# Where three normalizes stand in VectorE's queue: operand differences and an add moved ahead of them in the second chunks

## The chip, the cores and the metric

The kernel runs on one core of one Trainium2 chip. The metric is the device time of one execution in microseconds (us), as a median over several runs. TensorE does the matrix products, VectorE and ScalarE empty the accumulation banks (PSUM) and do the elementwise work, GpSimd and SyncE issue the transfers. Each engine works through its own queue in the order in which the program gives it its instructions. An instruction that waits holds up all that stands behind it on the same engine.

## The reference

Attention with projected keys and values, followed by a feed-forward layer with a squared ReLU:

```python
def _attn_ref(q, k, v, E, F):                 # q, k, v: 8 x 8 x 1024 x 64; E, F: 64 x 1024
    k_proj = np.einsum('ks,bhsd->bhkd', E, k)
    v_proj = np.einsum('ks,bhsd->bhkd', F, v)
    scores = np.matmul(q, k_proj.transpose(0, 1, 3, 2)) / np.sqrt(64)
    attn = softmax(scores)                    # over the 64 projected keys
    return np.matmul(attn, v_proj)

def _moe_ref(x, w_in, w_out):                 # x: 8192 x 512, w_in: 512 x 2048, w_out: 2048 x 512
    h = np.maximum(x @ w_in, 0.0)
    return h * h @ w_out
```

The heads of the attention's output are laid side by side as the 512 columns of `x`. Inputs and output are float32.

## The kernel before, in words

**Batches and chunks.** The outer loop runs over the eight batches b = 0 to 7. While TensorE does the feed-forward layer of batch b, pieces of the attention of batch b+1 (and a few of b+2) are put between its steps. A batch of 1024 tokens is two chunks of 512. The feed-forward work of a batch is a list of 62 steps, numbered from 0: for b of 1 and more these are 16 first-layer steps of chunk 0 (0 to 15), 15 second-layer steps of chunk 0 (16 to 30), then the same for chunk 1: first layer 31 to 46, second layer 47 to 61. The "second chunks" of this case are the steps 47 to 61.

**Order.** The order on every engine is written out by hand: instructions stand in each engine's queue in the order in which the program issues them. The dictionaries `PIECES` (batches 2 to 5), `BATCH_2` (used in batch 1's list), `LAST_PIECES` (batch 6) say ahead of which step each attention piece is issued. A piece at key n is issued just before step n.

**First layer.** A step is four matmuls of 128x512 into a bank. ScalarE takes the ReLU (lines 561 and 563), VectorE squares the result into `hsq` (line 571).

**Second layer.** The product of the 512 squared tokens with `w_out` is done with Strassen's scheme in Winograd's form: seven half-size products instead of eight. It needs four sums of blocks of `hsq`, called `s[0]` to `s[3]`, which VectorE makes in `sums` (line 521), each in two halves of four of the eight blocks: the low half (`q4` = 0) during the first layer, the high half (`q4` = 1) at its end or in the second layer. In this kernel they depend on one another: `s[1]` reads `s[0]`, `s[3]` reads `s[1]`, `s[2]` reads only `hsq`. Three are differences; `s[0]` is a sum. The products are the steps `p1` to `p7`, most of them split into a low and a high half (`lo`, `hi`), each half 8 matmuls of 128x256 (line 527). `p6` reads `s[1]`, `p5` reads `s[0]`, `p7` reads `s[2]`, `p3` reads `s[3]`. The orders of the second chunk are:

```python
# b = 1: steps 47 to 61
[p1a, p2a, p1b, p1c] + lohi(p5) + lohi(p6) + lohi(p3) + lohi(p7) + [p2b]  + lohi(p4)
# b = 2 to 6
[p1a, p2a, p1b, p1c, p2b] + lohi(p6) + lohi(p5) + lohi(p7) + lohi(p3)  + lohi(p4)
```

So for b = 2 to 6 step 51 is `p2b`, 52 and 53 are `p6`, 54 and 55 `p5`, 56 and 57 `p7`, 58 and 59 `p3`, 60 and 61 `p4`; for b = 1 step 48 is `p2a`, 49 `p1b`, 50 `p1c`, 51 and 52 `p5`, 53 and 54 `p6`, 55 and 56 `p3`, 57 and 58 `p7`, 59 `p2b`.

**Banks.** The products are accumulated in three banks called x, y and z. In batches 2 to 6 x and z are the same bank: `p2b` finishes x, VectorE's add (line 657, `o_sb` from `ps_z` and `p_a`) takes it into the output tile, and `p5` then starts z in that same bank. `p_a` is ScalarE's copy of y after `p1c` (line 651). y goes the same way: VectorE's add of y and `p_d` after `p7` frees y for `p4`.

**The attention pieces here.** `values g e` (line 258) multiplies the softmax's numerators with the projected values into a two-bank attention tile; `normalize g e` (line 285) multiplies that tile with the reciprocal sums `rs` on VectorE and writes a quarter of `xT`, the next batch's feed-forward input. A normalize frees its attention tile. In batch 1 there are two such tiles, so `values 1 0` and `values 1 1` (step 55) take the tiles that `normalize 0 0` and `normalize 0 1` read. From batch 2 on there are three.

Of the kernel before, what the change touches and what calls it, by code (L numbers as in the profile page):

```python
# [20 lines left out]
def kernel(  # L21
# [166 lines left out]
    class Attention:  # L188
# [262 lines left out]
            "+copy_vp, exponentials 2, +copy_kp",  # L451
        19: "exponentials 3", 20: "+copy_v_down", 21: "+transpose_q",
        27: "sums 0, sums 1, values 0 0, reciprocals 0", 28: "reciprocals 1", 29: "normalize 0 0",
        49: "values 0 1, values 1 0, values 1 1", 51: "normalize 0 1", 53: "normalize 1 0",
        55: "normalize 1 1",
    }
    LAST_PIECES = {
        18: "scores 0, scores 1, scores 2", 20: "exponentials 0, exponentials 1", 21: "exponentials 2",
        23: "scores 3, exponentials 3",
        27: "sums 0, sums 1, values 0 0, reciprocals 0", 28: "reciprocals 1", 29: "normalize 0 0",  # L460
        49: "values 0 1, values 1 0, values 1 1", 51: "normalize 0 1", 53: "normalize 1 0",
        55: "normalize 1 1",
    }
    BATCH_1 = {
# [10 lines left out]
        24: "scores 0, scores 1, exponentials 0", 25: "exponentials 1",  # L475
        27: "scores 2, scores 3, exponentials 2", 28: "exponentials 3",
        30: "sums 0, sums 1, logs 0", 31: "logs 1", 
        33: "+transpose_q, inverses 0", 36: "inverses 1", 47: "values 0 0, values 0 1", 48: "normalize 0 0, normalize 0 1",
        55: "values 1 0, values 1 1, +project 1", 56: "normalize 1 0",
        58: "+copy_kp", 59: "+copy_vp, normalize 1 1", 61: "+copy_v_down",  # L480
    }
# [22 lines left out]
    def ffn_groups(b, xT):  # L504
# [7 lines left out]
        def sums(hsq, s, q4, which):  # L512
            js = slice(4 * q4, 4 * q4 + 4)
            a11, a21 = hsq[:, 0, js, 0:TH], hsq[:, 0, js, TH:TCH]
            a12, a22 = hsq[:, 1, js, 0:TH], hsq[:, 1, js, TH:TCH]
            for o, x, y, op in (
                (0, a21, a22, ALU.add), (1, s[0][:, js], a11, ALU.subtract),
                (2, a11, a21, ALU.subtract), (3, a12, s[1][:, js], ALU.subtract),
            ):
                if o in which:  # L520
                    nc.vector.tensor_tensor(out=s[o][:, js], in0=x, in1=y, op=op)  # L521

        def product(ps, lhs, rhs, js, first=False, tbs=range(2)):

            for tb in tbs:
                for n, j in enumerate(js):
                    nc.tensor.matmul(  # L527
                        ps[tb] if len(ps) == 2 else ps[0][:, tb], lhsT=lhs[:, j, tb * P:(tb + 1) * P],
                        rhs=rhs[:, j], start=first and n == 0 and (tb == 0 or len(ps) == 2), stop=True,
                        skip_group_check=True,  # L530
                    )
# [3 lines left out]
        def chunk(ch):  # L535
# [49 lines left out]
            def operands(q4, which):  # L585
                sums(st["hsq"], st["s"], q4, which)
# [60 lines left out]
            def copy(to, name):  # L647
                if not (last and name == "y"):
                    used(f"ps_{name}")
                for ps, t in parts(st[name]):  # L650
                    nc.scalar.copy(to[:, t], ps)  # L651
# [18 lines left out]

            def p2a():
                if b:
                    operands(1, (1,) if b > 1 else (1, 3, 2))
                product(st["x"], st["A12"], W21, before, True)

            def p1b():
# [1 line left out]

            def p1c():
                product(st["y"], st["A11"], W11, range(7, 8))  # L680
                st["a"] = part_pool.tile([P, 2, MH], F32, name="p_a")
                copy(st["a"], "y")

# [51 lines left out]
            if 1 < b < B - 2 and ch == 0:  # L735
                second = [p1a, p1b, p1c, p2a, p2b] + lohi(p6) + lohi(p5) + lohi(p7) + lohi(p3)
            elif b == B - 1:
                (p5a, p5b), rest = lohi(p5), lohi(p7) + lohi(p3)
                second = [p1a, p2a, p5a, p1b, p1c, p2b] + lohi(p6) + [p5b] + rest
            elif b > 1:  # L740
                second = [p1a, p2a, p1b, p1c, p2b] + lohi(p6) + lohi(p5) + lohi(p7) + lohi(p3)
            else:
                second = [p1a, p2a, p1b, p1c] + lohi(p5) + lohi(p6) + lohi(p3) + lohi(p7) + [p2b]
# [88 lines left out]
```

## Time and profile before

| | |
|---|---|
| median of 4 runs | 482.97 us (482.19 to 484.17) |
| the profiled execution's own time | 483.14 us |
| its span | 481.4 us |
| granted TensorE clock | 0.999 |
| PE (TensorE's matmuls) busy | 468.3 us, 97% of the span |
| DVE (VectorE) busy | 314.2 us, 65% |
| ACT (ScalarE) busy | 247.8 us, 51% |
| POOL (GpSimd) busy | 34.9 us, 7% |

The profile is one execution of the program. PE is TensorE's matmul side and PEld its weight loads, DVE is VectorE, ACT is ScalarE, POOL is GpSimd, SP is SyncE. Matmuls are pipelined, and their ends in the profile are modelled: a row of 16 matmuls of 128x256 that run without a pause is listed as 1.91 us long, while the next such row starts 1.75 us after it. A pause of TensorE between two products is therefore best read from the distance of their starts, or from the chain, which lists a row from one end to the next. The chain is the path of work that ended last, followed back from the last instruction of the program; a step of it can be on any engine.

### The profile page before, as it was taken

The numbers are of one execution on the slowest core, as the hardware profiler recorded it, in microseconds if no ns is written. First come the engines' busy times: TensorE is split into PE (matmuls) and PEld (weight loads), VectorE is DVE, ScalarE is ACT, GpSimd is POOL, SyncE is SP. The second block draws the span as 40 slices with busy tenths as digits, with TensorE's granted clock in tenths as the row PEclk, the third lists the DMA queues.
The fourth block names the chain that finished last, engine by engine and source line by source line (L and its number), as shares of the span: only waits on it lengthen the run. The fifth ranks groups of instructions, "written<-read, shape, count | busy, mean of one in ns | idle before, by whom it ended". The sixth has DMA issues, their size and how long they took to land.

```text
span 481.4 us, 8400 instructions
## 1 busy us (share of the span) xinstructions
PE 468.3 (97%) x3630; PEld 293.9 (61%) x3630; DVE 314.2 (65%) x382; ACT 247.8 (51%) x365; POOL 34.9 (7%) x48
## 2 busy tenths in 40 slices
PE   3899999999999999999999999999999999999997
PEld 2544687475664756748475574846657475766656
DVE  1578955554957659584694837857485856949383
ACT  2377535758516574375633756156652666334352
POOL 6440020020020100001000100000000000000000
PEclk9999999999999999999999999999999999999999
DMA  9999989569979998209952199223401002020202
GB/s 163 203 204 207 154 187 200 139 111 221 159 125 238 141 205 149 88 1 143 229 78 89 14 182 213 43 87 58 130 1 75 13 1 88 1 89 0 89 1 87
DMA packets 72789, 55.46 MB, mean 115 GB/s; under 512 B 33968, under 2 KB 64944, under 8 KB 72752
## 3 DMA queue, kind: packets, MB, share of 16 engines
q0 software_dynamic: 30624, 29.36, 39.5%
q1 hardware_dynamic: 42128, 25.56, 21.0%
q8 instruction: 28, 0.46, 0.4%
q14 instruction: 9, 0.07, 0.0%
HBM read 59.24 MB, written 16.78 MB: 158 GB/s over the span
## 4 chain that ended last, share of the span: by engine, by line
PE 92%; DVE 4%; ACT 2%; DMA 1%; issue 0%; SPq 0%
PE ps_h L507 27%; PE ps_y L527 21%; PE ps_att L507 17%; PE ps_z L527 15%; PE ps_kv L216 2%; PE ps_att L527 2%; PE ps_att L258 2%; PE ps_att L243 2%; DVE hsq L571 1%; DMA e_f<-in_F_dram 1%; PE ps_x L527 1%; DVE s L521 1%; ACT h_relu L561 1%; PE ps_k L301 1%; DVE xT L285 0%; ACT expT L353 0%
## 5 line engine op out<-in xcount | busy, mean ns | idle before, releaser
L571 DVE TENSOR_TENSOR hsq<-h_relu 128x1024 bf16<-128x1024 f32 x123 | 149.9, 1222 | 79.1 <-ACT h_relu L563 62.5
L507 PEld LDWEIGHTS <-w_in 128*128 128x128 bf16 x1024 | 99.8, 98 | 117.6 <-issue 1.9
L507 PE MATMUL ps_h<-xT,w_in 128*128 128x512 bf16 x640 | 147.8, 379 | 0.2 <-DVE xT L390 0.2
L527 PEld LDWEIGHTS <-s 128*128 128x128 bf16 x1024 | 99.1, 98 | 17.2 <-issue 5.1
L561 ACT ACTIVATE h_relu<-ps_h 128x512 f32<-128x512 f32 x159 | 92.3, 596 | 24.0 <-PE ps_h L507 23.8
L507 PE MATMUL ps_att<-xT,w_in 128*128 128x512 bf16 x384 | 90.7, 379 | 0.0
L527 PEld LDWEIGHTS <-hsq 128*128 128x128 bf16 x768 | 73.8, 98 | 16.4 <-issue 6.0
L563 ACT ACTIVATE h_relu<-ps_att 128x1024 f32<-128x1024 f32 x48 | 49.2, 1024 | 55.4 <-PE ps_att L507 55.4
L527 PE MATMUL ps_y<-T,s 128*128 128x256 bf16 x480 | 57.8, 273 | 0.2
L521 DVE TENSOR_TENSOR s<-hsq 128x1024 bf16<-128x1024 bf16 x64 | 43.5, 683 | 0.0
L285 DVE TENSOR_TENSOR xT<-ps_att,rs 128x1024 bf16<-128x1024 f32 x28 | 33.4, 1215 | 0.9 <-PE ps_att L258 0.9
L657 DVE TENSOR_TENSOR o_sb<-ps_z,p_b 128x512 f32<-128x512 f32 x16 | 11.1, 692 | 33.1 <-PE ps_z L527 29.9
L527 PE MATMUL ps_z<-T,s 128*128 128x256 bf16 x256 | 30.9, 272 | 0.0
L527 PE MATMUL ps_z<-w_out,s 128*128 128x256 bf16 x256 | 30.6, 273 | 0.0
L527 PE MATMUL ps_y<-w_out,hsq 128*128 128x256 bf16 x240 | 30.5, 273 | 0.0
L651 ACT COPY o_sb<-ps_y 128x512 f32<-128x512 f32 x15 | 8.7, 580 | 40.2 <-PE ps_y L527 40.1
L527 PE MATMUL ps_y<-T,hsq 128*128 128x256 bf16 x240 | 29.0, 273 | 0.0
L250 ACT ACTIVATE expT<-ps_att 128x1024 bf16<-128x1024 f32 x28 | 27.7, 1028 | 1.9 <-PE ps_att L243 1.9
L657 DVE TENSOR_TENSOR o_sb<-ps_y,p_d 128x512 f32<-128x512 f32 x15 | 10.4, 690 | 23.1 <-issue 21.3
L651 ACT COPY p_b<-ps_y 128x512 f32<-128x512 f32 x15 | 8.8, 589 | 27.5 <-PE ps_y L527 27.5
L521 DVE TENSOR_TENSOR s<-s,hsq 128x1024 bf16<-128x1024 bf16 x32 | 21.8, 684 | 0.3
L521 DVE TENSOR_TENSOR s<-hsq,s 128x1024 bf16<-128x1024 bf16 x32 | 21.8, 683 | 0.0
(86 smaller groups left out, 277.4 us busy)
## 6 DMA issues: line engine op xcount, KB each, us to landing
out_dram<-o_sb SPq DMA_DIRECT2D x30, 512.0 KB, 3.2
K_sb<-in_k_dram POOLq DMA_DIRECT2D x7, 1024.0 KB, 10.4
V_sb<-in_v_dram POOLq DMA_DIRECT2D x7, 1024.0 KB, 17.5
Q_sb<-in_q_dram POOLq DMA_DIRECT2D x7, 1024.0 KB, 10.3
w_out<-in_moe_w_out_dram POOLq DMA_DIRECT2D x4, 512.0 KB, 13.2
w_in<-in_moe_w_in_dram POOLq DMA_DIRECT2D x7, 256.0 KB, 10.1
K_sb<-in_k_dram POOLq DMA_DIRECT2D x2, 512.0 KB, 9.1
out_dram<-o_sb SPq DMA_DIRECT2D x3, 256.0 KB, 2.1
```

Source lines behind the costliest of these rows:

```text
L216: nc.tensor.matmul(ps[0:KP, :], lhsT=ET[:, i, :], rhs=kv[:, :, i, :], start=f, stop=l)
L243: nc.tensor.matmul(ps[o, bank, :], lhsT=self.kT[r, 2 * pr + j, :], start=True, stop=True, rhs=self.qT[r, NT * (2 * pr + j):NT * (2 * pr + ...
L250: nc.scalar.activation(e[:], self.ps["s", pr][:], AF.Exp, scale=SCALE)
L285: nc.vector.tensor_tensor(out=self.xT[:, 2 * g + e].rearrange("p a n t -> p a (n t)"), in0=self.ps["v", g, e][:], in1=self.rs[g][:], op=AL ...
L507: nc.tensor.matmul(ps[:], lhsT=w_in_blk(cb, fb), rhs=xT[:, cb, :, 2 * ch:2 * ch + 2], start=(cb == 0), stop=(cb == NCB - 1),)
L521: nc.vector.tensor_tensor(out=s[o][:, js], in0=x, in1=y, op=op)
L527: nc.tensor.matmul(ps[tb] if len(ps) == 2 else ps[0][:, tb], lhsT=lhs[:, j, tb * P:(tb + 1) * P], rhs=rhs[:, j], start=first and n == 0 an ...
L561: nc.scalar.activation(r[:, n], ps[:], AF.Relu)
L563: nc.scalar.activation(r[:], st["h"][:], AF.Relu)
L571: multiply = lambda: nc.vector.tensor_tensor(out=o, in0=r[:], in1=r[:], op=ALU.mult)
L651: nc.scalar.copy(to[:, t], ps)
L657: nc.vector.tensor_tensor(out=to[:, t], in0=ps, in1=more[:, t], op=ALU.add)
```

## The change

In the second chunks of batches 1 to 6 VectorE gets the same instructions in another order. Nothing is added or removed, and the orders on TensorE, ScalarE, GpSimd and SyncE stay as they are. Of the waits, one kind changes sides: in batch 1 `values 1 0` and `values 1 1` now wait for VectorE itself, where before a wait of `p6` for `s[1]` ahead of them had covered it.

- Batches 2 to 6. Before: high `s[1]`, `normalize 0 1`, the add of x and `p_a` after `p2b`, high `s[2]`, high `s[3]`, `normalize 1 0`, `normalize 1 1`, the add of y and `p_d`. After: high `s[1]`, the add, high `s[2]`, high `s[3]`, then the three normalizes, then the add of y and `p_d`.
- Batch 1. Before: `normalize 0 0`, `normalize 0 1`, high `s[1]`, high `s[3]`, high `s[2]`. After: high `s[1]`, the two normalizes, high `s[3]`, high `s[2]`.

In chunk 0 of batch 1 the moved call gives VectorE the same order as before, since nothing else of VectorE's stands between.

```diff
 PIECES = {                                    # LAST_PIECES has the same change
-        49: "values 0 1, values 1 0, values 1 1", 51: "normalize 0 1", 53: "normalize 1 0",
+        49: "values 0 1, values 1 0, values 1 1", 52: "normalize 0 1", 54: "normalize 1 0",
         55: "normalize 1 1",
     }
 BATCH_2 = {
-        ... 47: "values 0 0, values 0 1", 48: "normalize 0 0, normalize 0 1",
+        ... 47: "values 0 0, values 0 1", 49: "normalize 0 0, normalize 0 1",
         55: "values 1 0, values 1 1, +project 1", 56: "normalize 1 0",
...
             def p2a():
                 if b:
-                    operands(1, (1,) if b > 1 else (1, 3, 2))
+                    operands(1, (1,))
                 product(st["x"], st["A12"], W21, before, True)
...
             def p1c():
                 product(st["y"], st["A11"], W11, range(7, 8))
+                if b == 1:
+                    operands(1, (3, 2))
                 st["a"] = part_pool.tile([P, 2, MH], F32, name="p_a")
                 copy(st["a"], "y")
```

## The prediction

> **What bounds the kernel now.** I read the page first, for the engine that fills the span.
>
> ```profile
> PE 468.3 (97%) x3630; PEld 293.9 (61%) x3630; DVE 314.2 (65%) x382; ACT 247.8 (51%) x365; POOL 34.9 (7%) x48
> PEclk9999999999999999999999999999999999999999
> PE 92%; DVE 4%; ACT 2%; DMA 1%; issue 0%; SPq 0%
> ```
>
> TensorE is busy for 97% of the span at full granted clock, and the chain that ended last runs on it for 92%. No matmul is changed, so the change can only be worth what TensorE now waits for, in the steps 47 to 61 of batches 1 to 6, because of what stands too early in VectorE's queue. DVE's 4% of the chain, some 19 us, is an invitation to hope for more; whether TensorE stood still in those 19 us is the next question. I went through the chain in order of time and looked for DVE rows beside steps 47 to 61. There is one place, in batch 1:
>
> ```profile
> 128.63 1.20 DVE s L521 x2
> 129.83 2.27 DVE xT L285 x2
> 132.09 0.61 DVE s L521
> 132.71 0.05 issue
> 132.75 1.05 PE ps_y L527 x8
> ```
>
> Two normalizes (L285), then the high `s[1]` (L521), and at once 8 matmuls into y: the high half of `p6`, which reads that `s[1]`. The chain runs on DVE from 122.19 to 132.70 us here. What TensorE lost in it is seen in the timeline of PE:
>
> ```profile
> 129.82 1.91 PE L527 MATMUL ps_z<-T,s 128*128 128x256 bf16 x16
> 131.57 2.23 PE L527 MATMUL ps_y<-T,s 128*128 128x256 bf16 x16
> ```
>
> Both rows are 16 matmuls of one shape; the first (`p5`) is an undisturbed 1.91 us, the second (`p6`) is 2.23. TensorE waited for 0.32 us, and no more, in a stretch where the chain names DVE for ten: until then it was working too, on matmuls that needed nothing of this queue.
>
> In batches 2 to 6 the chain names no DVE row in these steps, so I compared its PE pieces with one another (batch 4's second chunk):
>
> ```profile
> 304.70 1.75 PE ps_y L527 x16
> 306.45 1.82 PE ps_z L527 x16
> 308.27 1.75 PE ps_y L527 x16
> ```
>
> The second row is `p5`, and it takes 0.07 us more than its neighbours. The same 1.82 stands in the chain at 192.44, 249.44, 363.46 and 418.75, once in each of the five batches. The timeline of all engines around it says why:
>
> ```profile
> 303.43 0.59 ACT L651 COPY p_a<-ps_y 128x512 f32<-128x512 f32 x1 [2.50 <-PE ps_y L527]
> ...
> 303.89 0.69 DVE L521 TENSOR_TENSOR s<-s,hsq 128x1024 bf16<-128x1024 bf16 x1
> 304.50 1.22 DVE L285 TENSOR_TENSOR xT<-ps_att,rs 128x1024 bf16<-128x1024 f32 x1
> 304.54 1.91 PE L527 MATMUL ps_y<-T,s 128*128 128x256 bf16 x16
> 305.63 0.68 DVE L657 TENSOR_TENSOR o_sb<-ps_z,p_a 128x512 f32<-128x512 f32 x1
> 306.23 0.68 DVE L521 TENSOR_TENSOR s<-hsq 128x1024 bf16<-128x1024 bf16 x1
> 306.37 0.82 PE L527 MATMUL ps_z<-T,s 128*128 128x256 bf16 x6
> ```
>
> The add of x and `p_a` ends at 305.63 + 0.68 = 306.31, and `p5`, which takes over its bank, starts at 306.37. Without the wait it would start 1.75 after `p6`, at 306.29. In chunk 0 of the same batch, where no normalize stands ahead of the add, the two rows start 1.75 apart (276.71 and 278.46).
>
> **The change part by part.**
>
> *Batch 1.* The high `s[1]` takes the place of the two normalizes, at 129.75 by the timeline, and is ready 0.69 later, at 130.44. The high half of `p6` could start 8 matmuls of 1.75/16 each after 131.57, at 132.44. The cover is 2.0 us, so the whole 0.32 us goes. What is late next? The normalizes start 0.60 later (an `s` row frees the queue after 0.60), at 130.35 and 131.49, and the second ends at 132.70. `values 1 0` and `values 1 1`, which write over the tiles they read, start at 133.73 now and at 133.41 after the change: 0.7 us of slack. This is the one new wait, and matmuls alone are queued behind it. The high `s[3]` and `s[2]` begin and end where they did (133.22 + 0.68 = 133.90 for the last), because the sum ahead of them is the same; `p3`, their first reader, starts at 136.13. Gain 0.32 us.
>
> *Batches 2 to 6.* The add now stands right behind the high `s[1]`, whose slot ends at 304.50, but it must wait for `p2b`, whose last matmul ends at 304.70 (the chain row above starts there). A like handover, from `p3` to its add, takes 0.03 us (311.77 to 311.80), so the add runs from 304.73 to 305.42. That is 0.87 ahead of the 306.29 at which `p5` could start: the wait of 0.07 goes, five times, 0.35 us. In exchange DVE stands idle for 0.23 us where a normalize used to fill the wait for `p2b`. Queued behind it are `s[2]`, `s[3]` and all three normalizes. Their rows before:
>
> ```profile
> 306.83 0.68 DVE L521 TENSOR_TENSOR s<-hsq,s 128x1024 bf16<-128x1024 bf16 x1
> 307.43 2.35 DVE L285 TENSOR_TENSOR xT<-ps_att,rs 128x1024 bf16<-128x1024 f32 x2
> 310.11 0.69 DVE L657 TENSOR_TENSOR o_sb<-ps_y,p_d 128x512 f32<-128x512 f32 x1 [0.34 <-issue]
> ```
>
> After the change `s[2]` runs from 305.33, `s[3]` from 305.93, the normalizes from 306.53, 307.67 and 308.80 (starts 0.60 and 1.13 apart, as in the trace), and the last ends at 310.02 instead of 309.78. The add of y and `p_d` behind them must wait for `p7` anyway, whose row in the chain ends at 308.27 + 1.75 = 310.02, 0.09 ahead of that add; it keeps its place within 0.05. Its own cover is `p3`: `p4` takes y at 311.60, the add ends at 310.80. The next batch's first matmul, which reads `xT`, starts at 313.35, 3.3 us after the last normalize. So the idle 0.23 us costs TensorE nothing; without that cover it would cost 0.23 five times, 1.15 us. The product `p7`, which reads `s[2]`, starts at 308.11 and gains slack.
>
> One rule speaks against counting so tightly: "VectorE: DVE Perf Modes" in the Trainium skill, section "The DRAIN you can't avoid", says that the next VectorE operation cannot issue until the pipe is empty (it excepts some followers). Taken plainly the six operations of 0.69, 0.68, 0.68 and three times 1.22 would take 5.71 us from 304.73, to 310.44, and the add of y would end at 311.13, still ahead of `p4`; the trace has the starts closer than the durations (0.60 for 0.68, 2.35 for two normalizes of 1.21), and by either the sum stays the same.
>
> *A wait of `values` for VectorE* in place of TensorE's own is not in the trace. Bounds: below, nothing, since a wait that is long fulfilled only replaces one; a gain is excluded because no work goes. Above, 0.32 us, what the visible wait of `p6` cost. I take nothing, because it is fulfilled 0.7 us ahead, as the add-to-`p5` wait in chunk 0, which shows no pause.
>
> *Sum.* 0.32 + 5 x 0.07 = 0.67 us. The profiled execution of 483.14 becomes 482.47. It lies 0.17 above the median of 482.97, so on the median I expect 482.97 - 0.67 = 482.3 us, 0.14% less. A measurement of this kernel can tell about 0.3%, 1.45 us, from no change.
>
> **The rivals.**
>
> *The forecast*: the two kinds of pause go and nothing comes for them, 482.3 us. Chance 0.68.
>
> *The pauses stay or come back elsewhere* (the change does less than it says): the bank is held by something else than the add, or `p6` is next held by its own operands. For it: a pause of 0.07 is near what a start can scatter by. Against it: it recurs five times and is absent in chunk 0. 483.0 us. Chance 0.15.
>
> *The chain's DVE share was real*: the two normalizes' 2.27 us in batch 1's chain come off in full, and the five pauses too: 482.97 - 2.27 - 0.35 = 480.35 us. For it: the chain. Against it: TensorE's own rows show only 0.32 us of waiting there. It could be larger in executions that were not profiled, whose times spread over 2 us. Chance 0.11, scatter included.
>
> *Slower: the add at the head of the queue holds up the normalizes.* It waits for `p2b`, for ScalarE's `p_a` and for the earlier output transfer from its tile. If it starts a time d late, all behind it is late by d, and from d = 0.8 (`p4` at 311.60 against 310.80) TensorE pays d - 0.8 in each of five batches. At d = 1.3 that is 2.5, less the 0.32 of batch 1: 485.2 us. Against it: ScalarE's `p_a` copy ends at 303.43 + 0.59 = 304.02, ahead of `p2b`. Chance 0.06.
>
> **How the numbers follow.** Forecast and second case lie within 0.3% and give 0.83; the third is faster, 0.11; the fourth is slower, 0.06. The range goes from 481.2 to 483.6: the forecast's own scatter is that of the four runs, whose ends lie 0.8 below and 1.2 above their median, which gives 481.5 to 483.5 and takes in the case without effect; a little is added for the unknown wait of `values` (0.32). Left out are the ends of the third and fourth cases.
>
> **What would show it.** Right: the `p6` row of batch 1 falls from 2.23 to 1.91, the five `p5` pieces of the chain from 1.82 to 1.75, the `p_a` adds stand ahead of the normalizes with some 0.2 us of idle time before them, the chain no longer goes through L285 at 130 us. Wrong: a pause at `values` in batch 1 or at `p4` in batches 2 to 6, a normalize that ends near the next batch's first matmul, or PE rows as predicted and a time that moves by over 1 us.

## The result and the profile after

The changed kernel takes 482.23 us in the median (481.1 to 483.82, 50 runs), the kernel before 482.94 us (481.74 to 484.94, 75 runs). The ratio is 0.9986 with a 95% interval of 0.998 to 0.9992: 0.7 us less, a real difference and a small one. The profiled execution took 482.59 us, its span is 480.8 us.

From the page of the changed kernel, the busy times and the chain by engine:

```profile
PE 468.5 (97%) x3630; PEld 294.4 (61%) x3630; DVE 314.7 (65%) x382; ACT 247.7 (52%) x365; POOL 34.4 (7%) x48
PE 94%; ACT 2%; DVE 2%; DMA 1%; issue 0%; SPq 0%
```

The busy times are the same to 0.5 us. VectorE's share of the chain halved, from 4% to 2%, which would be some 10 us, and the time fell by 0.7. What left VectorE's share went to TensorE, which had run beside it: its own rose from 92% to 94%.

The timeline of PE in batch 1, `p5` and then `p6`:

```profile
129.94 1.91 PE L527 MATMUL ps_z<-T,s 128*128 128x256 bf16 x16
131.68 1.91 PE L527 MATMUL ps_y<-T,s 128*128 128x256 bf16 x16
```

The `p6` row went from 2.23 to 1.91 us. VectorE's timeline of that stretch has the high `s[0]` and `s[1]`, the two normalizes, then the high `s[2]` and `s[3]`:

```profile
129.26 0.68 DVE L521 TENSOR_TENSOR s<-hsq 128x1024 bf16<-128x1024 bf16 x1
129.97 0.69 DVE L521 TENSOR_TENSOR s<-s,hsq 128x1024 bf16<-128x1024 bf16 x1
130.59 2.35 DVE L285 TENSOR_TENSOR xT<-ps_att,rs 128x1024 bf16<-128x1024 f32 x2
132.85 0.68 DVE L521 TENSOR_TENSOR s<-hsq 128x1024 bf16<-128x1024 bf16 x1
133.45 0.68 DVE L521 TENSOR_TENSOR s<-hsq,s 128x1024 bf16<-128x1024 bf16 x1
```

The chain in batch 4's second chunk, in order of time (start, length, what):

```profile
304.35 1.75 PE ps_y L527 x16
306.10 1.75 PE ps_z L527 x16
307.85 1.75 PE ps_y L527 x16
```

The `p5` piece in the middle went from 1.82 to 1.75, and the same holds in the four other batches. VectorE's timeline of the same stretch:

```profile
303.54 0.69 DVE L521 TENSOR_TENSOR s<-s,hsq 128x1024 bf16<-128x1024 bf16 x1
304.45 0.69 DVE L657 TENSOR_TENSOR o_sb<-ps_z,p_a 128x512 f32<-128x512 f32 x1 [0.22 <-PE ps_z L527]
305.06 0.68 DVE L521 TENSOR_TENSOR s<-hsq 128x1024 bf16<-128x1024 bf16 x1
305.65 0.69 DVE L521 TENSOR_TENSOR s<-hsq,s 128x1024 bf16<-128x1024 bf16 x1
306.26 3.48 DVE L285 TENSOR_TENSOR xT<-ps_att,rs 128x1024 bf16<-128x1024 f32 x3
309.69 0.69 DVE L657 TENSOR_TENSOR o_sb<-ps_y,p_d 128x512 f32<-128x512 f32 x1
```

The add stands ahead of the normalizes, with 0.22 us of idle time before it that ends with TensorE's `p2b`. It ends at 305.14, and `p5` starts at 305.94, so 0.8 us of cover took the place of a wait. The add of y and `p_d` starts 2.01 us after `p7` does (307.68); before it was 2.00 (310.11 against 308.11).

### The profile page after: what moved, and what is told of

It is laid out like the page before. It is cut to its first block, busy times and chain, and to the rows that moved or that the text cites. A ratio compares the mean times of both kernels' runs of the same rounds, so it can differ in the third digit from the quotient of the medians.

```text
span 480.8 us, 8400 instructions
## 1 busy us (share of the span) xinstructions
PE 468.5 (97%) x3630; PEld 294.4 (61%) x3630; DVE 314.7 (65%) x382; ACT 247.7 (52%) x365; POOL 34.4 (7%) x48
## 4 chain that ended last, share of the span: by engine, by line
PE 94%; ACT 2%; DVE 2%; DMA 1%; issue 0%; SPq 0%
PE ps_h L507 28%; PE ps_y L527 22%; PE ps_att L507 17%; PE ps_z L527 15%; PE ps_att L258 2%; PE ps_kv L216 2%; PE ps_att L527 2%; PE ps_att L243 2%; PE ps_x L527 1%; DMA e_f<-in_F_dram 1%; PE ps_k L301 1%; ACT h_relu L561 1%; DVE hsq L571 1%; ACT expT L353 0%; DVE xT L390 0%; PE ps_fill L400 0%
```

## The experiments

The single executions of one kernel spread over some 3 us, and the effects at stake are 0.3 us. So beside each time I read the trace from a fixed step on: the start of `p4` in the first chunk of batch 1, up to which every engine has the same instructions in the same order in all ten kernels. What is left of the span from there is free of the opening of the program. The spans are taken to the hundredth, as the traces hold them.

| kernel | start of that `p4`, us | span, us | left, us | against before |
|---|---|---|---|---|
| before | 110.32 | 481.37 | 371.05 | |
| changed | 110.44 | 480.80 | 370.36 | -0.69 |
| batch 1 alone | 109.39 | 480.13 | 370.74 | -0.31 |
| batches 2 to 6 alone | 109.21 | 479.90 | 370.69 | -0.36 |
| add alone ahead | 110.56 | 480.92 | 370.36 | -0.69 |
| two normalizes ahead | 110.28 | 487.01 | 376.73 | +5.68 |
| one normalize more | 109.52 | 482.21 | 372.69 | +1.64 |
| two normalizes more | 109.34 | 488.34 | 379.00 | +7.95 |
| batch 1, two more | 111.05 | 483.18 | 372.13 | +1.08 |
| longer `p2b` | 109.58 | 479.89 | 370.31 | -0.74 |

Each row is one execution. The start of the fixed step scatters by 1.8 us over these ten. The ratios below are against runs of the kernel before that were taken beside each experiment, with a median of 483.16 us for the first four experiments and 483.14 for the others; each has its 95% interval behind it, and it is not simply the quotient of the two medians.

**Batch 1 alone**

```diff
-        ... 52: "normalize 0 1", 54: "normalize 1 0",     # both tables of batches 2 to 6
+        ... 51: "normalize 0 1", 53: "normalize 1 0",
```

> Only the batch-1 part of the change: the high s[1] ahead of the two normalizes; batches 2 to 6 in the old order. Forecast's theory (two separate pauses of TensorE): the p6 row of batch 1 falls from 2.23 to 1.91 us, the five p5 pieces stay at 1.82, 482.94 - 0.32 = 482.6 us. Rival (the chain's DVE share was real): 2.27 us come off, 480.7. Rival (the pause of p6 is held by something else): 482.9 and a p6 row of 2.23.

482.7 us against 483.16 of before, ratio 0.9989 (0.9973 to 1.0006). The time alone does not tell it from the kernel before; the rows do. `p6` in batch 1, from the timeline of PE:

```profile
130.64 1.91 PE L527 MATMUL ps_y<-T,s 128*128 128x256 bf16 x16
```

and a `p5` piece of batch 4 in the chain:

```profile
305.21 1.82 PE ps_z L527 x16
```

The pause of batch 1 is gone, and the five of 0.07 are there. The 2.27 us of normalizes, which this part took out of the chain, did not come off the time: from the fixed step on it is 0.31 us shorter.

**Batches 2 to 6 alone**

```diff
-        ... 49: "normalize 0 0, normalize 0 1",     # BATCH_2; p2a and p1c as before, too
+        ... 48: "normalize 0 0, normalize 0 1",
```

> Only the part in batches 2 to 6: the add, s[2] and s[3] ahead of the normalizes; batch 1 in the old order. Forecast's theory: the p6 row of batch 1 stays at 2.23 us, the five p5 pieces fall from 1.82 to 1.75, 482.94 - 0.35 = 482.6 us. Rival (the bank is held by something else than the add): five pieces of 1.82 and 482.9.

482.29 us, ratio 0.9984 (0.9971 to 0.9998). The mirror image: all `p5` pieces are 1.75, and in batch 1's `p6` the second half waits for `s[1]`:

```profile
130.46 1.04 PE L527 MATMUL ps_y<-T,s 128*128 128x256 bf16 x8
131.65 1.05 PE L527 MATMUL ps_y<-T,s 128*128 128x256 bf16 x8 [0.15 <-DVE s L521]
```

The second half starts 1.19 after the first instead of 0.87, so the pause is 0.32. The profile's own idle column shows 0.15 of it, because the modelled end of the first half reaches into the pause. Each part removes its own kind of pause and leaves the other kind, and from the fixed step on the two add up: 0.31 and 0.36 beside 0.69 for the whole. The medians of the two parts (0.46 and 0.87 less) are too scattered to show that.

**Two normalizes ahead of the add** (the kernel before, with more of the suspected cost)

```diff
-        ... 51: "normalize 0 1", 53: "normalize 1 0",
+        ... 51: "normalize 0 1, normalize 1 0",
```

> The kernel before with one more normalize (1 0) ahead of the add in batches 2 to 6, nothing else changed. If the add behind the normalizes holds up p5, it is 1.13 us later and so is p5: pieces of 1.82 + 1.13 = 2.95, five times 1.13 = 5.65 more, 488.6 us. If the 0.07 comes from anything else, p5 stays at 1.82 and the time at 482.9.

489.13 us (2 runs), ratio 1.0119 (1.0086 to 1.0152), 6.0 us more; from the fixed step on 5.68, where 5.65 was expected. In the timeline of PE, `p6` and `p5`:

```profile
306.77 1.91 PE L527 MATMUL ps_y<-T,s 128*128 128x256 bf16 x16
309.72 1.91 PE L527 MATMUL ps_z<-T,s 128*128 128x256 bf16 x16 [1.04 <-DVE o_sb L657]
```

`p5` starts 2.95 after `p6`, which is 1.75 + 1.20, and the profile names the add as what it waits for; the four other batches have 2.95 or 2.96. A normalize ahead of the add costs TensorE its full 1.13 us once the cover is used up. That rules out another holder of the bank.

**The add alone ahead**

```diff
 def p6(js):
+    if 1 < b < B - 1 and not js[0]:
+        operands(1, (2, 3))               # behind normalize 0 1
     product(st["y"], st["s"][1], T2[:], js)
...
 def p2b():
...
     add(st["o0"][:, :, 0:MH], "x", st["a"])
-    if b > 1:
+    if last or b == B - 1:
         operands(1, (2, 3))
```

> The changed kernel with the high s[2] and s[3] of batches 2 to 6 put back behind normalize 0 1; only the add stays ahead of it. If the add alone makes the gain, this equals the changed kernel: p5 pieces of 1.75, 482.2 us. If the operand differences matter too, p7 or p3 shows a pause and the time is above 482.2, by up to the 0.35 us that this part gained.

482.6 us, ratio 0.9984 (0.9966 to 1.0002); all `p5` pieces 1.75, no pause at `p7` or `p3`, and what is left of the span is that of the changed kernel to the hundredth (370.36 us). VectorE's order around the add:

```profile
304.57 0.69 DVE L657 TENSOR_TENSOR o_sb<-ps_z,p_a 128x512 f32<-128x512 f32 x1 [0.21 <-PE ps_z L527]
305.18 1.22 DVE L285 TENSOR_TENSOR xT<-ps_att,rs 128x1024 bf16<-128x1024 f32 x1
```

In batches 2 to 6 the gain is the add's place alone. That the operand differences moved too is worth nothing there, since their readers start later than either order makes them (here `s[2]` and `s[3]` end at 306.99 and 307.59, `p7` and `p3` start at 307.81 and 309.55).

**One normalize more, two more** (the changed kernel; the repeated ones write the same values again)

```diff
-        ... 52: "normalize 0 1", 54: "normalize 1 0",
+        ... 52: "normalize 0 1, normalize 0 1", 54: "normalize 1 0",     # or three times
```

> The changed kernel with normalize 0 1 issued twice in batches 2 to 6 (the second writes the same values again), which makes VectorE's queue behind the add 1.13 us longer. Forecast's theory, with the changed kernel's rows: the add of y and p_d starts 1.13 after 309.69 and ends at 311.51, p4 starts 0.06 later at 311.57 instead of 311.18: a pause of 0.39 in each of five batches, 482.23 + 1.95 = 484.2 us. If nothing of TensorE's hangs on this queue: 482.2. If the whole length is paid: 482.23 + 5.65 = 487.9.

> The same with normalize 0 1 issued three times, 2.26 us longer. Forecast's theory: past the cover each further us is paid in full, a pause of 0.39 + 1.13 = 1.52 at p4 in each of five batches, 482.23 + 7.6 = 489.8 us. If the cover were elastic, less than 7.6; if the whole length is paid, 11.3 and 493.5.

484.77 us, ratio 1.0035 (1.0018 to 1.0052), and 490.7 us (2 runs), ratio 1.0153 (1.0116 to 1.0189). `p3` and `p4` with one more, from the timeline of PE:

```profile
309.45 1.91 PE L527 MATMUL ps_z<-w_out,s 128*128 128x256 bf16 x16
311.66 1.91 PE L527 MATMUL ps_y<-T,hsq 128*128 128x256 bf16 x16 [0.31 <-DVE o_sb L657]
```

and with two more:

```profile
311.78 1.91 PE L527 MATMUL ps_z<-w_out,s 128*128 128x256 bf16 x16
315.25 1.91 PE L527 MATMUL ps_y<-T,hsq 128*128 128x256 bf16 x16 [1.56 <-DVE o_sb L657]
```

`p4` starts 2.21 after `p3`, a pause of 0.46 where 0.39 was expected. With two more it starts 3.47 after it, a pause of 1.72 where 1.52 was expected. Five times 0.46 and 1.72 are 2.3 and 8.6 over the changed kernel, and the column "left" has 2.33 and 8.64. So the cover at `p4` is there, it is some 0.8 us, and past it every further us is paid in full, as two lengths of queue show. What I had too small is the length of a repeated normalize, taken up below.

**Batch 1, two normalizes more** (the new wait of `values`)

```diff
-        ... 49: "normalize 0 0, normalize 0 1",
+        ... 49: "normalize 0 0, normalize 0 1, normalize 0 1, normalize 0 1",
```

> The changed kernel with normalize 0 1 of batch 1 issued three times (the same values again). It tests the new wait of values for VectorE: the last of the three ends 2.26 after 132.94, at 135.20; values 1 1 could start at 133.80 and starts at 135.26. Forecast's theory: a pause of 1.46 us inside the values row, 482.23 + 1.46 = 483.7 us. If values does not hang on it, 482.2.

484.8 us, ratio 1.003 (1.0015 to 1.0045). From VectorE's timeline and PE's:

```profile
131.20 4.86 DVE L285 TENSOR_TENSOR xT<-ps_att,rs 128x1024 bf16<-128x1024 f32 x4
```

```profile
134.13 0.41 PE L258 MATMUL ps_att<-expT,vp 64*32 64x512 bf16 x8
136.12 0.41 PE L258 MATMUL ps_att<-expT,vp 64*32 64x512 bf16 x8 [1.58 <-DVE xT L285]
```

`values 1 0` runs on time, and `values 1 1` starts 0.06 after the last normalize ends (131.20 + 4.86 = 136.06). Undisturbed it would follow the first by 0.28 us, half of the 0.56 that the chain of the changed kernel gives to the whole row. So the pause is 1.71 where 1.46 was expected, and from the fixed step on the span is 1.77 longer than the changed kernel's. The new wait is real; in the changed kernel it is fulfilled ahead of time.

**A longer `p2b`** (the changed kernel, one more pause taken by the same reading)

```diff
-            before = range(2) if (b, ch) == (0, 0) or 1 < b < B - 1 else lo
+            before = range(2) if (b, ch) == (0, 0) or 1 < b < B - 1 or (b, ch) == (1, 1) else lo
```

> The changed kernel, in the second chunk of batch 1 alone with p2 split after two blocks instead of four, so that p2b has 12 matmuls instead of 8 between p7 and p4. By the same reading the last small pause there (a p4 piece of 1.82 behind the add of y and p_d) goes to 1.75, and p5, p6 and values, which start 0.44 earlier, find their operands ready: 0.07 us less, 482.2, not to be told from the changed kernel by its time. If values is held by the normalizes (they end at 132.94, values would start at 133.08), the row behind p6 starts late.

482.2 us, ratio 0.9983 (0.9964 to 1.0002). The chain, `p2b` and `p4` of batch 1's second chunk:

```profile
138.30 1.31 PE ps_x L527 x12
139.61 1.75 PE ps_y L527 x16
```

`p4`, a piece of 1.82 in the changed kernel, takes 1.75, and nothing shows in its place: `values` starts at 132.22, 0.14 after the second normalize ends. The median cannot tell this from the changed kernel; the trace can.

## Why the prediction was right

**The sum.** 0.67 us were forecast, the medians differ by 0.71, and from the fixed step on the spans differ by 0.69. The two terms were tested apart: 0.32 in batch 1 and five times 0.07, each gone where its part of the change was made and there where it was not. That the bank was held by the add, which one rival doubted, is shown by the normalize that was put ahead of it and came out at the start of `p5`. That the forecast also met the median to 0.1 us was in part luck: it starts from the median of four runs that spread over 2 us, which happened to lie 0.03 us from that of 75.

**The chain's share as the gain.** That rival would have taken 2.6 us off. The halved DVE share of the chain beside 0.7 us of time, and batch 1 alone, whose 2.27 us of normalizes left the chain for 0.31 us of span, refute it.

**The held-up queue.** The slower rival's mechanism exists, as the added normalizes show: a pause at `p4` that grows with the queue behind the add, from about the forecast 0.8 us on. It did not come about because the add waits for 0.22 us (0.23 forecast), far from that point.

**The wait of `values`.** Taken at nothing, and nothing shows: `values` starts at 133.52, and the second normalize ends at 130.59 + 2.35 = 132.94. The slack is 0.58 us, where I had 0.7.

**Terms that were mis-sized, without effect on the sum.** I let the high `s[1]` of batch 1 start as soon as a `s` row frees the queue, 0.60 after the one ahead. It starts 0.71 after it (129.26 to 129.97), because it reads what that one writes and so begins when that has ended: `s[3]`, of the same shape, reads nothing of the `s[2]` ahead of it and starts 0.60 after it (132.85 to 133.45). The trace of before had the longer spacing in its other batches (303.17 to 303.89). It is what cost the slack of `values` 0.1 us, and why the high `s[2]` and `s[3]` did not quite keep their places: the last ends at 134.13, where 133.90 and the 0.11 by which `p6` starts later in this execution give 134.01. `p3`, which reads it, starts at 135.93. (In batch 1 the loop in `sums` makes `s[2]` ahead of `s[3]`, in both kernels, whatever order the call names; the description of the change has the two the other way round. Nothing in the sum depends on it.) The add's handover from `p2b` took 0.10 us (304.35 to 304.45) instead of the 0.03 of its model row.

**A repeated normalize.** The repeated normalizes in my expectations were 1.13 us apart, as those on different tiles are; on the same tile a repeat costs more. With one more, the add of y starts 4.66 us after the first normalize (306.27 to 310.93) instead of 3.43 (306.26 to 309.69), so 1.23 us for the repeat; with two more 5.92 (308.60 to 314.52), so 2.49 for two. That is 0.10 and 0.23 over the 1.13 and 2.26 I had taken, which is the 0.07 and 0.20 that the pauses at `p4` exceeded their expectation by, to 0.03. By the lengths of the rows (3.48, 4.74 and 6.00 us for three, four and five normalizes) a repeat is 1.26 us; the start of the add in the changed kernel is not set by the queue alone, since `p7` ends only 0.10 ahead of it (309.59 in the chain). In batch 1 the row of four took 4.86 us, where 2.35 and two of 1.13 make 4.61, and that 0.25 is what the pause of `values` was over. That it is the second write to the same tile that waits for the first was argued from the code, not tried.

The same rows bear on "VectorE: DVE Perf Modes" in the Trainium skill, section "The DRAIN you can't avoid": it says that the next operation does not start until the pipe is empty, and that one that is not held starts earlier. If the end of a row is taken for the moment at which the pipe is empty, the dependent pairs keep to the first (0.71 between starts for a row of 0.68) and the independent ones to the second (0.60 for 0.68, 1.13 for 1.21). What the page counts as held was not tried here.

## What to carry to other kernels

In a queue that is served in order, put the instruction that frees a bank or makes an operand for the bound engine ahead of longer work that nobody needs yet, even if the queue then idles a little; and count the cover of what falls back behind it, since past that cover each us is paid in full. Price such a change by the pauses of the bound engine (distances of starts of like rows), never by another engine's share of the chain. Where the executions scatter by more than the effect, compare the traces from a step on that lies ahead of the change.

## What the runs showed of the hardware that I had not expected

In these ten executions the scatter sits in the opening. They reach the same step of batch 1, after the same instructions, between 109.21 and 111.05 us. From there to the end each differs from the kernel before by its pauses alone, to 0.1 us. The scatter is there even earlier: the first matmuls of the first layer (line 507) start between 19.95 and 22.34 us, and from them to that step eight of the ten take 88.71 or 88.72 us, the two that start first 88.99 and 89.26. What makes the first 22 us vary was not tried.
